# The first-token row and the first group's Newton steps on GpSimd instead of VectorE in an attention, Fourier-mix and FFN kernel

## The chip, the cores and the metric

The kernel runs on one core of a Trainium2 chip. The core has TensorE (PE, matmuls; PEld is its weight load), VectorE (DVE), ScalarE (ACT), GpSimd (POOL) and SyncE (SP, whose queue issues nearly all DMAs). Each engine works through its own instructions in the order in which they were put there; engines wait for each other by semaphores. The metric is the device time of one execution in microseconds (us); a shorter time is better.

## The reference

Input q, k, v of 4 batches, 8 heads, 768 tokens, head size 64; weights 512x2048 and 2048x512. All of it is float32.

```python
scores = scale * q @ k.T                       # per batch and head
keep = (pos_k < n_sink) | (0 <= pos_q - pos_k < window)     # 4 sink tokens, window 128
a = softmax(where(keep, scores, -1e9));  x = a @ v          # (4, 768, 512)
X = fft(fft(x, axis=1), axis=2);  u = x + real(X)
un = (u - mean(u)) / sqrt(var(u) + 1e-6)       # per token, over 512 features
out = u + relu(un @ w_ch1) @ w_ch2
```

## The kernel before

**Stages.** Each batch has six blocks of 128 tokens. The attention walks over 24 blocks x 4 pairs of heads = 96 steps, one step per pair of heads, about 2 us each, in the batch order of the program 0, 1, 2, 3. A step's chain is: PE scores (L703) into one of two PSUM buffers `s`; DVE merges the older keys (L709) and takes mask and row minimum (`soft1`, L721, twice per pair), which also frees the PSUM buffer; ACT takes the exponential (L727); PE transposes (L755, `pt`); ACT copies the result to SBUF (L762, `pta`); POOL cuts the window's edge out of it, once into a new tile (L771, `ptl`) and once in place (L779, `pta`); PE multiplies with v (L793, `xt`); DVE writes the block of x (`store_x`, L821) with the inverse sums (L743), which read what POOL prepared (L747, `mx`). POOL also makes the sink's two-part probabilities (L738, L739, `sk`).

**Fourier.** When four blocks of a batch are there, `fourier` books that batch's transform into later steps. Rows are folded (n against 768 - n, then m against 512 - m: L352, L359, L362, shared by DVE and POOL; in the last batch by DVE alone), split into two parts (L365 on ACT, L368 on DVE: `gh`, `gl`), multiplied with DFT constants on PE (stage 1, L395, results `za`, `zr`, `zb`, split again at L402 and L410; stage 2, L422 and L443), combined on DVE (L448, L449) and added to x (L459, L460, on POOL; in the last two batches also on DVE).

**The first token's row.** Token 0 takes no part in the fold; its attention row is worked out apart, goes through DRAM and comes back as `xr` in 33 partitions (`load_row`, L347). Then, once for each batch: `put_row` (L381) copies it into block 3 (`u[NHALF][0:1]`) once the first fold has read that block, `mid_sum` (L372) folds it, `mid_row` (L376, L378) splits it into `sph`, which the last matmul of stage 1 reads. They stand 5, 8 and 10 steps behind the start of the batch's folds (`ROW`), behind the step's other bookings for their engine.

**The first group's variance.** The FFN works on groups of blocks; the first has four (blocks 0 to 3 of batch 0). `normalize` books its statistics (steps 64 on), `deviations` (steps 72 to 80; the variance of 128 rows x 4 blocks becomes 1/sqrt by one integer guess, L522 and L524, and four Newton rounds of three operations, L527, L529, L531), `un_make` (from step 81 on, L539), the transposes and the two-part split (L545 to L554, `un_slots`).

**What sets the order.** Up to step 96 the order on each engine is written out (`SCHEDULE`: for each step, what comes in which order; a letter stands for the step's bookings for that engine). From step 97 (`CUT`) to the end of the first FFN group a scheduler sets the order; into that stretch fall the last batch's transform, the last attention blocks, the weights' conversion (`convert`, L591 to L593 on DVE, L608 on ACT, L609 on POOL) and the first FFN group (L620 and L1126 on PE). The rest of the FFN is again in written order.

Of the kernel before, what the change touches and what calls it, by code (L numbers as in the profile page):

```python
# [16 lines left out]
ALU = mybir.AluOpType  # L17
# [8 lines left out]
NHALF = NB // 2  # L26
# [8 lines left out]
NR = 33  # L35
# [28 lines left out]
F_N, F_M, F_S, ROW = (3, 3), (4, 5), (6, 7), (5, 8, 10)  # L64
# [142 lines left out]
def kernel(  # L207
# [17 lines left out]
    def f32(ap):  # L225
        return ap.bitcast(F32)
# [44 lines left out]
    def run(general):  # L271
        tag = "g" if general else ""
        with ExitStack() as p1:
# [8 lines left out]
            def at(s, eng, fn):  # L282
                ev.setdefault((s, eng), []).append(fn)
# [49 lines left out]
            def fourier(b, at, ready):  # L333
                u = uview(b)
# [32 lines left out]
                def fold_lo(j):  # L367
                    V.tensor_tensor(gl[:, j], t_.pop(("g", j)), f32(gh[:, j]), op=ALU.subtract)  # L368

                def mid_sum():  # L370
                    r = t_["x0"]
                    V.tensor_tensor(r[:, 1:256], r[:, 1:256], r[:, 511:256:-1], op=ALU.add)  # L372

                def mid_row():
                    t = t_["x0"]
                    V.tensor_copy(sph[:NR, :257], t[:, :257])  # L376
                    lo = sph[NR - 1:NR, :257]
                    V.tensor_tensor(lo, t[NR - 1:NR, :257], f32(lo), op=ALU.subtract)  # L378

                def put_row():  # L380
                    V.tensor_copy(u[NHALF][0:1], t_["x0"][0:1])  # L381

# [83 lines left out]
                for j in range(NHALF):  # L466
# [8 lines left out]
                    at(k + F_S[1], "V", lambda j=j: fold_lo(j))  # L475
                at(ready[0] + ROW[0], "V", put_row)
                at(ready[0] + ROW[1], "V", mid_sum)
                at(ready[0] + ROW[2], "V", mid_row)
                k = ready[2] + S1
# [37 lines left out]

            def deviations(b, blk, n):

# [5 lines left out]
                for _ in range(4):  # L525
                    yield
                    V.scalar_tensor_tensor(t, y, -0.5, x, op0=ALU.mult, op1=ALU.mult)  # L527
                    yield
                    V.tensor_tensor(t, t, y, op=ALU.mult)  # L529
                    yield  # L530
                    V.scalar_tensor_tensor(y, t, 1.5, y, op0=ALU.add, op1=ALU.mult)  # L531

# [26 lines left out]
            def normalize(s0, s1, s2, get_bank):  # L559
# [4 lines left out]
                for i in range(n):  # L564
                    at(s0 + 2 * i, "V", lambda i=i: stats(0, i, u[i], i, (0, 0)))
                steps = deviations(0, 0, n)
                for i in range(14):
                    at(s1 + i * (s2 - s1) // 14, "V", lambda: next(steps, None))
                for i in range(n):
# [769 lines left out]
```

## Time and profile before

| | us |
|---|---|
| time, median of 3 runs | 784.29 (782.91 to 787.69) |
| time of the profiled execution | 786.08 |
| its span, first to last instruction | 784.1 |
| PE busy | 755.7 (96%) |
| DVE busy | 453.5 (58%) |
| ACT busy | 237.1 (30%) |
| POOL busy | 185.1 (24%) |

The profiled execution lies 1.8 us above the median; 2.0 us of it lie around the span. Busy shares over the whole span say little here: the attention and the transforms fill the first 280 us, in which all engines work, and the FFN the rest, in which PE does nearly everything. So the stretches are read apart, by windows. PE's busy time takes the modelled ends of pipelined matmuls in, so that idle time of PE that does show is time in which nothing ran.

### The profile page before, as it was taken

What the parts mean: (1) busy time and instruction counts of PE and PEld (TensorE: products, weight loads), DVE (VectorE), ACT (ScalarE), POOL (GpSimd) and SP (SyncE); (2) the same over time, 40 slices, a digit from 0 to 9 for tenths busy, and PEclk for the clock granted to TensorE, in tenths of its full rate; (3) what the DMA queues carried; (4) which work ended last, traced back from release to release, by engine and by line L of the source; (5) the groups of instructions that cost most, each with busy time, mean ns of one, the idle gap of its engine ahead of it and who ended that gap; (6) DMA issues with size and microseconds to landing.
All of it is one profiled execution on the core that took longest, in us unless ns stands there. A gap on an engine that the chain in (4) does not pass through costs nothing.

```text
span 784.1 us, 11917 instructions
## 1 busy us (share of the span) xinstructions
PE 755.7 (96%) x4379; PEld 616.8 (79%) x4379; DVE 453.5 (58%) x1330; ACT 237.1 (30%) x704; POOL 185.1 (24%) x307
## 2 busy tenths in 40 slices
PE   7999998989998999999999999999999999999996
PEld 5676876867777878899888888888888888888895
DVE  6878587999999489561456424661456424611211
ACT  4887765766523123221111101111111111110110
POOL 2567477477654255100000000000000000000000
PEclk9999999999999899999999999999999999999998
DMA  9863535434215266110100002000200001000100
GB/s 283 268 177 105 151 83 177 127 112 145 86 50 166 92 196 208 66 59 1 54 0 1 1 18 89 1 0 1 81 0 1 2 1 54 1 0 1 54 1 31
DMA packets 41810, 57.67 MB, mean 74 GB/s; under 512 B 2796, under 2 KB 27500, under 8 KB 41360
## 3 DMA queue, kind: packets, MB, share of 16 engines
q1 hardware_dynamic: 41456, 53.07, 21.6%
q0 software_dynamic: 288, 3.76, 1.3%
q8 instruction: 36, 0.59, 0.3%
q14 instruction: 30, 0.25, 0.1%
HBM read 47.37 MB, written 9.45 MB: 72 GB/s over the span
## 4 chain that ended last, share of the span: by engine, by line
PE 80%; DVE 9%; POOL 4%; issue 3%; ACT 2%; DMA 2%; SPq 1%; POOLq 0%; DVEq 0%; ACTq 0%
PE o L1126 33%; PE h L620 33%; PE s L703 3%; PE xt L793 3%; PE pt L755 2%; PE za L395 1%; DVE cv L592 1%; DVE cv L593 1%; DVE sm L721 1%; PE zb L395 1%; ACT pta L762 1%; ACT sm L727 1%; DMA vt<-in_v_sink_dram 1%; POOL ptl L771 1%; DVE s L709 1%
## 5 line engine op out<-in xcount | busy, mean ns | idle before, releaser
L1126 PE MATMUL o<-w,h 128*128 128x512 f32 x876 | 218.6, 397 | 0.0
L1119 DVE SCALAR_TENSOR_TENSOR h<-h,h 128x512 fp32r<-128x512 f32 (+1 forms) x107 | 65.4, 611 | 250.5 <-ACT h L1114 250.3
L1126 PEld LDWEIGHTS o<-w,h 128*128 128x128 f32 x876 | 164.5, 190 | 36.0
L1114 ACT ACTIVATE h<-h 128x512 fp32r<-128x512 f32 (+1 forms) x107 | 57.1, 534 | 368.6 <-PE h L620 362.4
L620 PE MATMUL h<-un_slots,w 128*128 128x512 f32 (+1 forms) x576 | 124.7, 365 | 0.0
L620 PEld LDWEIGHTS h<-un_slots,w 128*128 128x128 f32 x576 | 99.6, 188 | 19.6
L620 PE MATMUL h<-un_last,w 128*128 128x512 f32 (+1 forms) x432 | 89.0, 355 | 0.0
L620 PEld LDWEIGHTS h<-un_last,w 128*128 128x128 f32 x432 | 72.7, 188 | 12.8
L727 ACT ACTIVATE sm<-sm,mx 128x132 f32<-128x132 f32 x192 | 76.0, 400 | 6.0 <-DVE mx L721 6.0
L1150 DVE STREAM_TRANSPOSE unf<-un 32x128 f32<-32x128 f32 x224 | 67.7, 302 | 3.2
L703 PE MATMUL s<-ring,q 64*128 64x260 f32 x320 | 49.9, 418 | 8.9 <-DVE mx L721 5.3
L721 DVE CUSTOM_DVE_ANT_0 sm<-s,mask 128x132 f32<-128x132 f32 x192 | 48.5, 293 | 6.3 <-PE s L701 1.3
L703 PEld LDWEIGHTS s<-ring,q 64*128 64x128 f32 x320 | 27.3, 188 | 21.6 <-issue 8.0
L609 POOL TENSOR_TENSOR w<-cv,w 128x512 fp32r<-128x512 f32 x25 | 34.1, 1366 | 30.5 <-ACT w L608 30.5
L793 PE MATMUL xt<-ptl,ldv 128*64 128x128 f32 x384 | 39.3, 285 | 0.2 <-POOL ptl L771 0.2
L727 ACT ACTIVATION_READ_ACCUMULATOR sm<-sm,mx 128x1 f32 x192 | 36.7, 191 | 0.0
L1126 PE MATMUL o<-w_ring,h 128*128 128x512 f32 x144 | 35.6, 393 | 0.0
L762 ACT COPY pta<-pt 128x512 f32<-128x512 f32 x48 | 28.0, 583 | 24.9 <-PE pt L755 23.5
L709 DVE COPY_PREDICATED s<-older,s 128x256 f32<-128x256 uint8 x80 | 33.7, 421 | 1.6 <-PE s L703 1.6
L771 POOL TENSOR_SCALAR_AFFINE_SELECT ptl<-pta 128x512 f32<-128x512 f32 x48 | 32.5, 678 | 7.3 <-ACT pta L762 7.2
L793 PEld LDWEIGHTS xt<-ptl,ldv 128*64 128x64 f32 x384 | 21.9, 136 | 15.1 <-issue 6.2
L793 PE MATMUL xt<-pta,ldv 128*64 128x128 f32 x320 | 31.7, 274 | 0.3 <-POOL pta L779 0.3
(197 smaller groups left out, 1039.4 us busy)
## 6 DMA issues: line engine op xcount, KB each, us to landing
raw<-in_moe_w_ch_dram SPq DMA_DIRECT2D x32, 512.0 KB, 3.7
ldv<-in_v_dram SPq DMA_DIRECT2D x28, 256.0 KB, 3.3
ring<-in_qk_dram SPq DMA_DIRECT2D x24, 264.0 KB, 4.8
out_dram<-u SPq DMA_DIRECT2D x24, 256.0 KB, 2.1
q<-in_qk_dram SPq DMA_DIRECT2D x20, 256.0 KB, 4.4
cst<-in_dft_dram POOLq DMA_DIRECT2D x1, 3348.0 KB, 12.8
ud<-us SPq DMA_DIRECT2D x12, 256.0 KB, 2.1
u<-ud SPq DMA_DIRECT2D x2, 1024.0 KB, 4.9
```

The lines of the kernel that those rows point to most:

```text
L620: T.matmul(ps[:, :tb], a[:, cs], x[:, :, cc, :], start=n == 0, stop=n == 3 * NCC - 1)
L703: T.matmul(ps[:, j, :P + W], st["q", g][rows, hp, :], keys(g, 2 * hp + j), start=True, stop=True)
L709: V.copy_predicated(ps[:, :, P + NS:P + W], older[qi > 2], ps[:, :, 0:P])
L721: V.tensor_tensor_reduce(sm[:, h % 4], ps[:, j, P:P + W], mask[min(qi, 3)], -SCALE, 3.0e38, ALU.add, ALU.min, accum_out=mx[:, 0, h:h + 1])
L727: A.activation(sm[:, h % 4], sm[:, h % 4], AF.Exp, bias=mx[:, 0, h:h + 1], scale=-1.0, accum_out=mx[:, 1, h:h + 1])
L762: A.copy(a, st.pop(("pt", g, hp // 2)))
L771: G.affine_select(lo, a, [[0, 4], [s, P]], compare_op=ALU.is_ge, fill=0.0, base=0, channel_multiplier=-s)
L793: T.matmul(ps[D * j:D * j + D, p, :], st["v", kb(g) - i][:, h, :], a[:, h % 4, :], start=i == 0, stop=i == n - 1)
L1114: A.activation(h[0], ps[:, :tb], AF.Relu)
L1119: V.scalar_tensor_tensor(h[1], ps[:, :tb], 0.0, f32(h[0]), op0=ALU.max, op1=ALU.subtract)
L1126: T.matmul(po[i], a[:, ts_], x, start=f == 0 and n == 0, stop=f == NF - 1 and n == 2)
L1150: V.transpose(unf[32 * q:32 * q + 32, :, r], un[r].rearrange("p (c q j) -> p c q j", c=NCC, q=4)[:, :, q])
```

## The change

`put_row`, `mid_sum` and `mid_row` are made by GpSimd, in the same steps, in all four batches. The twelve Newton operations of the first group are made by GpSimd too. The two fused operations of a round (scalar_tensor_tensor) are written with operations that GpSimd has: L527 becomes one tensor_tensor, L531 a tensor_scalar and a tensor_tensor, so a round has four instructions instead of three. The integer guess stays on VectorE, as do the deviations of the other groups and the general path.

```diff
+                R = V if general else G
+
                 def mid_sum():
                     r = t_["x0"]
-                    V.tensor_tensor(r[:, 1:256], r[:, 1:256], r[:, 511:256:-1], op=ALU.add)
+                    R.tensor_tensor(r[:, 1:256], r[:, 1:256], r[:, 511:256:-1], op=ALU.add)
 
                 def mid_row():
                     t = t_["x0"]
-                    V.tensor_copy(sph[:NR, :257], t[:, :257])
+                    R.tensor_copy(sph[:NR, :257], t[:, :257])
                     lo = sph[NR - 1:NR, :257]
-                    V.tensor_tensor(lo, t[NR - 1:NR, :257], f32(lo), op=ALU.subtract)
+                    R.tensor_tensor(lo, t[NR - 1:NR, :257], f32(lo), op=ALU.subtract)
 
                 def put_row():
-                    V.tensor_copy(u[NHALF][0:1], t_["x0"][0:1])
+                    R.tensor_copy(u[NHALF][0:1], t_["x0"][0:1])
...
-                at(ready[0] + ROW[0], "V", put_row)
-                at(ready[0] + ROW[1], "V", mid_sum)
-                at(ready[0] + ROW[2], "V", mid_row)
+                at(ready[0] + ROW[0], "V" if general else "G", put_row)
+                at(ready[0] + ROW[1], "V" if general else "G", mid_sum)
+                at(ready[0] + ROW[2], "V" if general else "G", mid_row)
...
-            def deviations(b, blk, n):
+            def deviations(b, blk, n, eng=V):
...
                     yield
-                    V.scalar_tensor_tensor(t, y, -0.5, x, op0=ALU.mult, op1=ALU.mult)
+                    if eng is V:
+                        V.scalar_tensor_tensor(t, y, -0.5, x, op0=ALU.mult, op1=ALU.mult)
+                    else:
+                        G.tensor_tensor(t, y, x, op=ALU.mult)
                     yield
-                    V.tensor_tensor(t, t, y, op=ALU.mult)
+                    eng.tensor_tensor(t, t, y, op=ALU.mult)
                     yield
-                    V.scalar_tensor_tensor(y, t, 1.5, y, op0=ALU.add, op1=ALU.mult)
+                    if eng is V:
+                        V.scalar_tensor_tensor(y, t, 1.5, y, op0=ALU.add, op1=ALU.mult)
+                    else:
+                        G.tensor_scalar(t, t, -0.5, 1.5, op0=ALU.mult, op1=ALU.add)
+                        G.tensor_tensor(y, t, y, op=ALU.mult)
...
-                steps = deviations(0, 0, n)
+                steps = deviations(0, 0, n, V if general else G)
                 for i in range(14):
-                    at(s1 + i * (s2 - s1) // 14, "V", lambda: next(steps, None))
+                    at(s1 + i * (s2 - s1) // 14, "V" if i < 2 or general else "G", lambda: next(steps, None))
```

Over the program DVE has 28 instructions less, POOL 32 more; the order on SP is the same, and on PE and ACT it differs only in the stretch that the scheduler orders. (The changed kernel's line numbers are 2 higher from `fourier` on, 9 higher behind `deviations`.)

The first place is POOL's order in the middle of the Newton rounds (`stat` is the tile of mean and variance), in the attention of batch 2. Before, three instructions stand between the last `sk` of a half block and the next:

```order
L738 CAST sk_2272<-sm_0_2167 128x2x16
L739 TENSOR_TENSOR sk_2272<-sm_0_2167,sk_2272 128x2x16
L771 AFFINE_SELECT ptl_3_2300<-pta_3_2266 128x512
L352 TENSOR_TENSOR f_2_0_2302<-u_65 128x512
L779 AFFINE_SELECT pta_3_2266<-pta_3_2266 128x512
L738 CAST sk_2272<-sm_2_2240 128x2x16
```

Of the change:

```order
L747 CAST sk_2271<-sm_0_2167 128x2x16
L748 TENSOR_TENSOR sk_2271<-sm_0_2167,sk_2271 128x2x16
L532 TENSOR_TENSOR stat_0_1899<-stat_0_1899 128x4
L534 TENSOR_TENSOR stat_0_1899<-stat_0_1899 128x4
L780 AFFINE_SELECT ptl_3_2300<-pta_3_2267 128x512
L539 TENSOR_SCALAR stat_0_1899<-stat_0_1899 128x4
L540 TENSOR_TENSOR stat_0_1899<-stat_0_1899 128x4
L352 TENSOR_TENSOR f_2_0_2304<-u_65 128x512
L788 AFFINE_SELECT pta_3_2267<-pta_3_2267 128x512
L532 TENSOR_TENSOR stat_0_1899<-stat_0_1899 128x4
L534 TENSOR_TENSOR stat_0_1899<-stat_0_1899 128x4
L747 CAST sk_2271<-sm_2_2239 128x2x16
```

So the rounds' instructions stand in pairs ahead of `ptl`, of the fold `f` and of `sk`; three of the eight pairs are in this piece.

The second place is POOL's order where `mid_row` of batch 1 falls, among the updates `u` of batch 0. Before:

```order
L459 TENSOR_TENSOR u_64<-u_64,d_1_1662 128x257
L460 TENSOR_TENSOR u_64<-u_64,d_1_1662 128x255
L771 AFFINE_SELECT ptl_3_1798<-pta_3_1765 128x512
L352 TENSOR_TENSOR f_1_2_1800<-us_2_1076,us_5_1079 128x512
L779 AFFINE_SELECT pta_3_1765<-pta_3_1765 128x512
```

Of the change:

```order
L461 TENSOR_TENSOR u_64<-u_64,d_1_1662 128x257
L462 TENSOR_TENSOR u_64<-u_64,d_1_1662 128x255
L378 CAST sph<-xr_1449 33x257
L380 TENSOR_TENSOR sph<-xr_1449,sph 1x257
L780 AFFINE_SELECT ptl_3_1798<-pta_3_1765 128x512
L352 TENSOR_TENSOR f_1_2_1800<-us_2_1076,us_5_1079 128x512
L788 AFFINE_SELECT pta_3_1765<-pta_3_1765 128x512
```

The two instructions of `mid_row` now stand ahead of `ptl`, a fold and `pta`; in batch 0 they stand ahead of the same three.

The third place is POOL's order where the scheduler has put the last batch's row. Before:

```order
L779 AFFINE_SELECT pta_3_3053<-pta_3_3053 128x512
L460 TENSOR_TENSOR u_65<-u_65,d_2_3141 128x255
L459 TENSOR_TENSOR u_65<-u_65,d_2_3141 128x257
```

Of the change:

```order
L788 AFFINE_SELECT pta_3_3057<-pta_3_3057 128x512
L383 COPY us_3_2624<-xr_3032 1x512
L374 TENSOR_TENSOR xr_3032<-xr_3032 33x255
L378 CAST sph<-xr_3032 33x257
L380 TENSOR_TENSOR sph<-xr_3032,sph 1x257
L462 TENSOR_TENSOR u_65<-u_65,d_2_3145 128x255
L461 TENSOR_TENSOR u_65<-u_65,d_2_3145 128x257
```

All four instructions stand together, behind the attention's last window cut and ahead of the updates.

## Rows read from the trace of the kernel before

**Rows 1.** Windows: us; per engine busy (xcount); granted PE clock, DMA share, GB/s.

```profile
100.00:140.00 40.00, 36.20 (x307) 27.61 (x307) 32.09 (x117) 24.99 (x95) 28.62 (x55) 1.00 0.49 148
140.00:164.00 24.00, 22.88 (x217) 18.55 (x214) 23.23 (x96) 16.77 (x63) 14.65 (x27) 1.00 0.32 92
164.00:181.00 17.00, 14.29 (x125) 10.70 (x123) 16.47 (x61) 11.44 (x43) 13.55 (x26) 1.00 0.40 128
200.00:254.00 54.00, 49.01 (x297) 41.31 (x295) 53.53 (x88) 19.91 (x45) 31.57 (x27) 1.00 0.33 106
254.00:261.00 7.00, 6.16 (x18) 5.24 (x19) 1.47 (x3) 1.73 (x4) 1.28 (x1) 0.51 0.27 92
280.00:784.00 504.00, 497.38 (x2353) 412.71 (x2351) 224.03 (x544) 77.37 (x141) 20.89 (x17) 1.00 0.10 34
```

**Rows 2.** PE's waits over the span: us in total, times, longest.

```profile
PE s L703 <- DVE mx L721: 5.3, 10, 2.6
PE a L422 <- DVE zb L410: 2.6, 1, 2.6
```

**Rows 3.** DVE's groups by form, 146.6 to 163 us: the first group's Newton operations.

```profile
L531 DVE SCALAR_TENSOR_TENSOR stat<-stat 128x4 f32<-128x4 f32 x4 | 2.5, 613 | 0.0
L529 DVE TENSOR_TENSOR stat<-stat 128x4 f32<-128x4 f32 x4 | 2.2, 546 | 0.1
L527 DVE SCALAR_TENSOR_TENSOR stat<-stat 128x4 f32<-128x4 f32 x4 | 1.1, 276 | 0.0
```

**Rows 4.** Timelines of POOL and of DVE (start, duration), around 153 us.

```profile
152.45 1.27 POOL L352 TENSOR_TENSOR f<-u 128x512 f32<-128x512 f32 x1
...
152.54 1.21 DVE L531 SCALAR_TENSOR_TENSOR stat<-stat 128x4 f32<-128x4 f32 x1
```

**Rows 5.** The row's operations by tile: ns min/median/max, first and last start.

```profile
L372 DVE TENSOR_TENSOR xr<-xr x4: 404/408/419, 60.2 to 212.8; 33x255 f32<-33x255 f32 x4
L376 DVE CAST sph<-xr x4: 281/296/722, 63.1 to 221.3; 33x257 fp32r<-33x257 f32 x4
L378 DVE TENSOR_TENSOR sph<-xr,sph x4: 417/418/737, 63.4 to 222.7; 1x257 fp32r<-1x257 f32 x4
L381 DVE COPY u<-xr x2: 404/406/408, 53.8 to 157.7; 1x512 f32<-1x512 f32 x2
L381 DVE COPY us<-xr x2: 405/406/408, 101.6 to 212.1; 1x512 f32<-1x512 f32 x2
```

**Rows 6.** POOL's groups by form: busy us, mean ns of one, idle before.

```profile
L771 POOL TENSOR_SCALAR_AFFINE_SELECT ptl<-pta 128x512 f32<-128x512 f32 x48 | 32.5, 678 | 7.3 <-ACT pta L762 7.2
...
L738 POOL CAST sk<-sm 128x32 fp32r<-128x32 f32 x48 | 11.5, 239 | 53.6 <-ACT sm L727 53.5
...
L359 POOL TENSOR_TENSOR f<-f 128x255 f32<-128x255 f32 x9 | 6.6, 738 | 0.8 <-DVE f L362 0.3
L747 POOL TENSOR_SCALAR mx<-mx 128x8 f32<-128x8 f32 x24 | 6.4, 265 | 2.0
```

**Rows 7.** Chain that ended last, 112 to 127 us: start, us, what.

```profile
112.29 0.22 POOL sk L738
...
126.11 0.60 POOL u L460
...
126.74 0.70 DVE bn L515
```

**Rows 8.** POOL's timeline in three places, idle time before in brackets.

```profile
64.01 0.66 POOL L738 CAST sk<-sm 128x32 fp32r<-128x32 f32 x1 [1.07 <-ACT sm L727]
...
67.12 0.82 POOL L779 TENSOR_SCALAR_AFFINE_SELECT pta<-pta 128x512 f32<-128x512 f32 x1
...
112.29 0.21 POOL L738 CAST sk<-sm 128x32 fp32r<-128x32 f32 x1 [2.14 <-ACT sm L727]
...
216.31 1.85 POOL L460 TENSOR_TENSOR u<-u,d 128x255 f32<-128x255 f32 x1 [4.43 <-DVE d L448]
```

**Rows 9.** PE's timeline: the matmul that reads that `pta`, and one at 254 us.

```profile
68.00 0.44 PE L793 MATMUL xt<-pta,ldv 128*64 128x128 f32 x4
...
254.84 1.66 PE L422 MATMUL a<-cst,za 128*128 128x258 f32 x6 [2.62 <-DVE zb L410]
```

**Rows 10.** DVE's timeline ahead of that matmul.

```profile
253.16 1.15 DVE L593 SCALAR_TENSOR_TENSOR cv<-raw,cv 128x512 int32<-128x512 int32 x1
254.23 0.55 DVE L410 TENSOR_TENSOR zb<-zb,zb 128x386 fp32r<-128x386 f32 x1
```

## The prediction

> **What bounds the kernel now.** I read the windows first, to see which stretch can move at all. From 280 us on PE works 497 of 504 us [rows 1]; none of the moved operations runs there, so that stretch only starts earlier or later. Before it, PE idles little: 3.8 us of 40 from 100 to 140, 1.1 of 24 to 164, 2.7 of 17 from 164 to 181, 5.0 of 54 from 200 to 254 [rows 1]. What DVE is relieved of can give back no more than such idle time, and only what DVE causes of it. PE's waits name DVE as the chief cause: 5.3 us in ten waits for the PSUM buffer that L721 frees, 2.6 us in one wait for L410 [rows 2]. DVE is full in 140 to 181 and 200 to 254 (39.7 of 41, and 53.5 of 54 us), POOL is not (28.2 of 41, 31.6 of 54) [rows 1]. That speaks for the change.
>
> Then I read DVE's and POOL's timelines side by side, because a busy DVE may be a waiting one. The Newton operation L531 at 152.54 has four numbers in each partition and takes 1.21 us; it ends at 153.75, POOL's fold, begun at 152.45, at 153.72 [rows 4]. The twelve operations take 5.8 us together (2.5, 2.2, 1.1), between 276 and 613 ns each on the mean of their line [rows 3], although they are all one size. So a DVE operation of this kind stands until the POOL instruction that began before it is through. That speaks against the change: what is put on POOL becomes something that DVE's other two-input operations (folds, splits, conversions) stand behind.
>
> The chain shows where POOL itself decides: from 112.29 to 126.71 it runs through POOL's instructions alone, until DVE's L515 at 126.74 [rows 7].
>
> **The change, part by part.** The sum is made against the profiled execution (786.1 us, 1.8 above the median of the runs).
>
> *Removed from DVE.* Four times `put_row` 0.41, `mid_sum` 0.41, `mid_row` 0.30 + 0.42 us: 1.53 us per batch, 6.1 in all at the medians [rows 5]; twelve Newton operations, 5.8 us [rows 3]. Together 11.9 us.
>
> *Added to POOL.* No row shows these forms there except one. `mid_sum` has the form of L359 but for fewer partitions: 0.74 us; the subtraction over 257 elements in one partition: the same 0.74. The copy of 512 elements lies between 0.27 (L747, 8 elements) and 0.68 (L771, 512): 0.68, by its length. The cast of 257 lies between 0.24 (L738) and 0.68: the middle, 0.46 [rows 6]. That is 2.6 us per batch (2.0 to 2.8), 10.5 in all. A Newton instruction on four elements lies between nothing and 0.68; the nearest row is L747 with 0.27 on eight, so sixteen take 4.3 us (0 to 10.9). Together 14.8 us.
>
> The Trainium skill's page "SBUF — State Buffer", section "Who interferes with whom", states that GpSimd and a VectorE instruction with two SBUF inputs exclude each other for whole instructions, and that whoever issues first blocks the other; the pair of rows at 152 us agrees (1.21 us for four elements). By that rule the move trades 11.9 us of DVE's time, part of it waiting, for 14.8 us in which POOL can block DVE; were this all, the sum would be +2.9 us instead of the one below.
>
> *Newton stretch and batch 2, 140 to 181.* POOL has 9.4 us free from 140 to 164 [rows 1], more than the 4.3 + 0.7 us it gets, and the result is wanted by L539 only in step 81. So nothing waits for it, and DVE loses 5.8 us of work ahead of the stretch in which PE idles 2.7 us [rows 1]. All of that is the most that can be won; nothing, if the folds behind the Newton operations stand behind POOL instead. I take two thirds, -1.8 us (0 to -2.7), since what is removed is twice the idle time. The row's own four operations of batch 2 I put at 0: POOL idles 3.4 us of the 17 from 164 to 181 [rows 1]; without that cover, +1.2.
>
> *Batch 1.* `put_row` and `mid_sum` come before POOL's 2.14 us of waiting that end at 112.29 [rows 8], and hide in them (1.42 us). `mid_row` stands in the run that the chain follows, ahead of `ptl`, a fold and `pta`: 0.46 + 0.74 = +1.2 us (0 if DVE's L515 has other cover, 2.6 if nothing hides).
>
> *Batch 0.* `mid_row` stands behind the `sk` at 64.01 and ahead of the `pta` cut that ends at 67.94; PE takes it at 68.00 [rows 8, 9], so there is no slack. +1.2 us, less what the cast at 64.01 gains when DVE's own two instructions are gone (0.66 against a mean of 0.24, [rows 6, 8]): +0.5 us (0 to 0.8). `put_row` and `mid_sum` fall ahead of POOL's 1.07 us of waiting.
>
> *Batch 3 and the conversion.* DVE is the bound there. It gives up 1.9 us (the cast took 0.72 here, [rows 5]). POOL takes its 2.6 us in 4.4 us of idle time ahead of 216.31 [rows 8], so no update is late; but DVE's folds, splits and conversions run at that very time and stand behind it. I take half of POOL's time as DVE's loss: -1.9 + 1.3 = -0.6 us (-1.9 to +0.7). It comes off the 2.62 us for which PE waits at 254.84 for L410 [rows 9, 10].
>
> *Sum.* -1.8 + 1.2 + 0.5 - 0.6 = -0.7 us: 785.4 us for an execution like the profiled one, **783.6 us** against the median. What is late next is the same as before: the scores' buffer in the attention, L410 at the end of the last transform.
>
> The page "GPSIMD Engine Reference" of the Trainium skill, section "Instruction dispatch", gives some 6 us, shown by no instruction of the profile, for the first call of a freshly loaded GpSimd kernel. A plain copy is new to POOL here; would it load one, the sum by that page would be up to +5.3 us. The trace of before cannot show it, since POOL makes no such copy there; it is no term of the sum.
>
> **Rivals.**
> 1. *The wait at 254.84 closes.* The clock granted to PE falls to 0.51, the lower of its two levels (1.2 instead of 2.4 GHz), from 254 to 261 us, just after PE had stood 2.62 us [rows 1, 9]. If DVE comes 2.6 us earlier, the 2.0 us that the forecast leaves of the wait go, and with them perhaps the low clock, worth 7 x 0.49 = 3.4 us: 783.6 - 2.0 - 3.4 = 778.2. For it: DVE is full all through. Against it: POOL's 2.6 us fall among DVE's two-input operations.
> 2. *The port is what counts.* The trade as the skill's rule has it, as a mechanism of this kernel: every new POOL instruction costs DVE its length where DVE is full. +2.9 us, 787.2. For it: the 1.21 us at 152.54 [rows 4]. Against it: before 140 us DVE isn't full (32.1 of 40, [rows 1]).
> 3. *Slower: POOL's queue decides.* Each `ptl` and `pta` behind a new instruction comes later, and PE with it. With nothing hidden that is 3 x 2.6 + 4.3 = 12.1 us, 796.4. It is slower by over 1% when 7.8 of the 12.1 us are not hidden. For it: the chain through POOL and the missing slack at 68.00 [rows 7 to 9]. Against it: POOL waits for ACT before it in most places (1.07 and 2.14 us, [rows 8]) and has 11.4, 9.4 and 3.4 us free in the three windows from 100 to 181 us [rows 1].
> 4. *Nothing is moved off any path*: the relief is hidden as the cost is, 784.3.
>
> **How the numbers follow.** Chances: the forecast, with rival 4 inside its own range of 781.5 to 786, 0.58; rival 1 0.14; rival 2 0.15; rival 3 0.10; anything else 0.03. 1% is 7.8 us, about what a measurement of this kernel can tell from no change: under 776.5 lies only a rival 1 that wins more than its 5.4 us (0.05); over 792.1 the greater part of rival 3 (0.07); within 1% 0.88. The range reaches from rival 1's 778.0 to 789.5, which is the sum with no relief at 140 to 181 and the upper bounds of the others (783.6 + 1.8 + 1.4 + 0.3 + 1.2 + 1.3 = 789.6); it leaves out rival 3's whole price and the far end of rival 1.
>
> **What would show it.** In the changed profile: the row's operations on POOL at about 0.7, 0.7, 0.5 and 0.7 us, the sixteen at about 0.3; DVE's busy time down by about 10 us; PE's idle time from 164 to 181 under 2.7 us; the run of POOL around 112 to 127 us longer by about 1; PE's wait for L410 around 254 us still there at 1 to 3 us, with the low clock behind it. The prediction is wrong if a POOL instruction on four elements takes over 0.5 us, if `pta` or `ptl` become PE's chief wait, or if the wait at 254 us and the low clock are gone.

## The result

The changed kernel is slower: **787.82 us** (median of 20 runs, 786.01 to 790.13) against 784.58 us (782.21 to 787.69) on the same chip, ratio 1.0043, 95% interval 1.0033 to 1.0053. That is 2.6 to 4.2 us lost where a gain of 0.7 was forecast. The time lies inside the range of 778.0 to 789.5 and within 1% of before, but it moved the other way than the forecast said. The profiled execution spans 785.7 us.

### The profile page after: what moved, and what is told of

Read it like the earlier page. It is cut to its first block, busy times and chain, and to the rows that moved or that the text cites. A ratio compares the mean times of both kernels' runs of the same rounds, so it can differ in the third digit from the quotient of the medians.

```text
span 785.7 us, 11920 instructions
## 1 busy us (share of the span) xinstructions
PE 757.0 (96%) x4379; PEld 619.1 (79%) x4379; DVE 448.6 (57%) x1302; ACT 236.8 (30%) x704; POOL 194.7 (25%) x339
## 4 chain that ended last, share of the span: by engine, by line
PE 81%; DVE 9%; ACT 3%; POOL 3%; issue 2%; DMA 1%; SPq 0%; DVEq 0%; ACTq 0%; POOLq 0%
PE o L1135 32%; PE h L629 32%; PE xt L802 4%; PE s L712 4%; PE pt L764 2%; PE za L397 2%; DVE cv L601 1%; DVE cv L602 1%; ACT pta L771 1%; PE zb L397 1%; ACT sm L736 1%; DVE cv L600 1%; DVE sm L730 1%; PE a L424 1%; DMA vt<-in_v_sink_dram 1%
## 5 line engine op out<-in xcount | busy, mean ns | idle before, releaser
L1135 PEld LDWEIGHTS o<-w,h 128*128 128x128 f32 x876 | 162.8, 188 | 35.5
L712 PE MATMUL s<-ring,q 64*128 64x260 f32 x320 | 49.3, 417 | 6.2 <-DVE mx L730 2.8
L730 DVE CUSTOM_DVE_ANT_0 sm<-s,mask 128x132 f32<-128x132 f32 x192 | 48.4, 292 | 8.0 <-PE s L710 3.1
L712 PEld LDWEIGHTS s<-ring,q 64*128 64x128 f32 x320 | 27.6, 188 | 17.9 <-issue 5.6
```

Source lines behind the costliest of these rows:

```text
L712: T.matmul(ps[:, j, :P + W], st["q", g][rows, hp, :], keys(g, 2 * hp + j), start=True, stop=True)
L730: V.tensor_tensor_reduce(sm[:, h % 4], ps[:, j, P:P + W], mask[min(qi, 3)], -SCALE, 3.0e38, ALU.add, ALU.min, accum_out=mx[:, 0, h:h + 1])
L1135: T.matmul(po[i], a[:, ts_], x, start=f == 0 and n == 0, stop=f == NF - 1 and n == 2)
```

## The profile after

In the changed kernel lines are 2 higher from `fourier` on and 9 higher behind `deviations`: L703, L721, L779 and L410 of before are L712, L730, L788 and L412 here, and the row's operations are L374, L378, L380 and L383. Kernels of the experiments with lines added are higher by a few more. From the page (busy us, share, instructions):

```profile
PE 757.0 (96%) x4379; PEld 619.1 (79%) x4379; DVE 448.6 (57%) x1302; ACT 236.8 (30%) x704; POOL 194.7 (25%) x339
```

The windows that answer to [rows 1], with the same columns:

```profile
100.00:140.00 40.00, 36.97 (x299) 28.64 (x297) 28.86 (x110) 24.06 (x89) 29.87 (x56) 0.91 0.43 131
140.00:164.00 24.00, 22.95 (x211) 18.76 (x209) 19.31 (x86) 17.39 (x67) 16.27 (x45) 1.00 0.42 119
164.00:181.00 17.00, 14.68 (x133) 11.25 (x130) 16.33 (x48) 10.06 (x39) 16.04 (x26) 1.00 0.35 114
200.00:254.00 54.00, 48.59 (x292) 41.86 (x293) 53.33 (x88) 19.82 (x47) 31.14 (x32) 0.97 0.28 88
254.00:261.00 7.00, 6.19 (x34) 5.22 (x33) 5.35 (x6) 3.10 (x7) 4.35 (x3) 1.00 0.67 225
```

The relief arrived: DVE works 19.3 us from 140 to 164 where it worked 23.2 [rows 1]. PE hardly used it: 22.95 us of 24 there, 22.88 before. The low clock at 254 to 261 is gone (1.00, 0.51 before), but there is one in the window from 100 to 140 (0.91) and one in that from 200 to 254 (0.97), where before there was none.

PE's waits over the span (us in total, times, longest), to be read against [rows 2]:

```profile
PE s L712 <- DVE mx L730: 2.8, 7, 0.7
PE xt L802 <- POOL pta L788: 2.7, 3, 1.4
PE za L397 <- ACT asb L433: 2.4, 1, 2.4
```

The wait for DVE halved (5.3 to 2.8 us), but most of that is not the change's. Half of the 5.3 us was one wait at 15 us, in the first block, before any operation that was moved:

```profile
15.02 2.13 PE L703 MATMUL s<-ring,q 64*128 64x260 f32 x8 [2.57 <-DVE mx L721]
```

The same place costs 0.56 us in the changed kernel and also in e11, which is the kernel before up to its Newton steps; so it differs between executions. From 46 us on the wait for DVE fell from 2.8 to 1.9 us. Waits for POOL's `pta` and for ACT's `asb` came instead.

Here is one such place in batch 0 and the same in batch 1: POOL's timeline, the matmul of PE that reads `pta`, and DVE's two waits that follow in batch 1 (start, duration, what; in brackets the idle time before it and what ended it).

```profile
65.12 0.39 POOL L378 CAST sph<-xr 33x257 fp32r<-33x257 f32 x1
...
68.39 0.63 POOL L788 TENSOR_SCALAR_AFFINE_SELECT pta<-pta 128x512 f32<-128x512 f32 x1
...
69.07 0.44 PE L802 MATMUL xt<-pta,ldv 128*64 128x128 f32 x4 [1.38 <-POOL pta L788]
...
118.12 0.86 POOL L378 CAST sph<-xr 33x257 fp32r<-33x257 f32 x1
...
121.93 0.63 POOL L788 TENSOR_SCALAR_AFFINE_SELECT pta<-pta 128x512 f32<-128x512 f32 x1
...
122.61 0.69 PE L802 MATMUL xt<-pta,ldv 128*64 128x128 f32 x4 [0.97 <-POOL pta L788]
...
125.98 0.20 DVE L752 RECIPROCAL mx<-mx 128x8 f32<-128x8 f32 x1 [2.64 <-POOL mx L756]
...
128.55 0.69 DVE L517 BATCH_NORM_STATS2 bn<-u 128x6 f32<-128x512 f32 x1 [2.37 <-POOL u L462]
```

In batch 0 PE took `pta` at 68.00 without a wait [rows 9]; now it stands 1.38 us. In batch 1 it stands 0.97 us for the same cut. DVE's wait for POOL's `mx` there was 0.70 us before and is 2.64 now; its wait for `u` is as long as before (2.38), and bn, which ended POOL's run at 126.74 [rows 7], starts at 128.55. About 0.7 us of that is the lag with which the changed kernel comes to 111 us (111.39 against 110.70 for PE's `x<-vs` matmul of the table below).

**Where PE stands.** To place each loss I took the start of PE's `x<-vs` matmuls, one for each block of the attention (the 24 rows of L807 in PE's timeline, L816 after). The table gives each kernel's lag against the kernel before at five of them, in us, set to zero at 46 us, ahead of the first place that mid_row touches; "low clock" is where the granted clock reads 0.5, the lower of its two levels (1.2 in place of 2.4 GHz), between 46 and 280 us. Each line is one execution.

```
kernel             at 74   at 111  at 138  at 194  at 215  low clock
before              0       0       0       0       0      254-261
after              +1.05   +0.95   +2.48   +2.60   +3.54   122-129, 232-235
e1 Newton only     +0.40   +0.45   +0.48   +0.15   +1.55   208-211, 259-262
e2 row only        +2.66   +3.67   +4.84   +4.26   +5.23   69-72, 233-236
e3 mid_row back    +0.37   +0.29   +0.29   +0.45   +1.74   204-207
e4 mid_row later   +0.21   +0.93   +3.54   +3.87   +4.82   133-136, 232-235
e5 mid_row early   +1.48   +1.42   +1.64   +1.75   +2.69   none
e6 mid_row b1      +0.37   +0.31   +1.48   +1.70   +3.09   206-209
e7 mid_row b0      +1.07   +1.00   +1.03   +1.21   +2.15   none
e8 mid_row b2,b3   +0.40   +0.29   +0.32   +0.49   +1.46   none
e9 placed          +0.53   +0.80   +0.98   +1.12   +2.07   229-233
e10 POOL more      +1.09   +1.08   +3.95   +3.96   +3.96   132-136, 259-262
e11 Newton one     +0.05   +0.30   +0.32   +0.07   +1.41   205-208, 256-260
e12 free only      +0.03   -0.09   +0.21   +0.38   +0.60   120-124
e13 batch 3 only   +0.04   -0.14   -0.18   -0.14   +0.81   none
e14 batch 3 back   +2.55   +4.09   +5.22   +5.29   +5.28   68-72, 260-263
```

The changed kernel loses 1.05 us in batch 0 (by 74), 1.5 in batch 1 (by 138), nothing that shows in batch 2, 0.95 in batch 3 (between 194 and 215).

Not all that moves a stand is the change. Kernels that are the same up to a place differ there by up to 0.4 us (e11 +0.30, e13 -0.14 at 111). Waits for DMA differ: before 111 us PE waits 1.2 us for one in the kernel before, 2.2 in e2 and 2.8 in e14; the 1.0 and 1.6 us more are what these two lose between 74 and 111. And a low clock moves the stand by itself: e1 and e11 have nothing moved in batch 3 and lose 1.4 us between 194 and 215, with a low clock there.

## The experiments

Each median is of 8 to 13 runs; the kernel before stood at 784.2 to 784.6 us beside them, and each ratio is to the kernel before on the same chip. In the expectations a theory is what was held to be so, a rival what speaks against it; their letters are explained where they first stand (C is one thing in e6 to e8 and another in e11).

**Which part loses: e1, e2, e3.** e1 moves only the Newton steps, e2 only the row's operations:

```
e1:  R = V                                      # the row's operations, steps booked on "V"
e2:  steps = deviations(0, 0, n)                # Newton steps on VectorE
```

> The first-token row's operations stay on VectorE; only the sixteen Newton instructions are on GpSimd. Theory M (PE waits for the window cut `pta`, because `mid_row` stands ahead of it on POOL in batches 0 and 1): 783.5 to 785.0 us, no different from before within 0.1%, since nothing of `mid_row` is on POOL. Rival N (the Newton instructions on POOL are what costs): 786.5 to 788. Rival P (every instruction moved to POOL costs VectorE its length, wherever it stands): about +1 us for 4.3 of the 14.8 us moved, 785.6.

> Only the row's operations (four per batch) are on GpSimd, the Newton steps are on VectorE as before. Theory M: the whole loss, 787 to 788.5 us. Rival N: 784 to 785.2. Rival P: 10.5 of the 14.8 us moved, so about +2.3 us, 786.9.

Measured: e1 784.07 us (ratio 0.9992, 0.9978 to 1.0006), e2 787.46 us (1.0037, 1.0025 to 1.0050). The loss is in the row's operations; the Newton steps show no loss, and a gain of up to 1.7 us is not excluded by e1's time alone (its stand, and e11, settle that). e3 puts only `mid_row` back:

```
- R.tensor_copy(sph[:NR, :257], t[:, :257])
+ V.tensor_copy(sph[:NR, :257], t[:, :257])
- R.tensor_tensor(lo, t[NR - 1:NR, :257], f32(lo), op=ALU.subtract)
+ V.tensor_tensor(lo, t[NR - 1:NR, :257], f32(lo), op=ALU.subtract)
- at(ready[0] + ROW[2], "V" if general else "G", mid_row)
+ at(ready[0] + ROW[2], "V", mid_row)
```

> The change with `mid_row` alone (cast and subtraction, four batches) back on VectorE; `put_row`, `mid_sum` and the Newton steps stay on GpSimd. Theory M: 784 to 785.3 us, PE no longer waits for `pta` at 67 and 122 us. Rival P: 4 x 1.4 + 4.3 = 9.9 of 14.8 us still moved, about +2.1 us, 786.7. Rival N: 786.5 to 788.

Measured: 784.34 us (1.0009, 0.9993 to 1.0025). Eight of the sixteen row operations and all Newton operations are on POOL here and cost nothing that shows (0.37 us by PE's stand at 74, see below), so theory P falls, whose 786.7 lies outside the interval. PE has no wait for `pta` left at 67 and 122 us. `mid_row` makes the loss.

**Is it the place: e4, e5.** The same line with mid_row's step at 12, behind `pta`, and at 8, directly behind `mid_sum`:

```
- F_N, F_M, F_S, ROW = (3, 3), (4, 5), (6, 7), (5, 8, 10)
+ F_N, F_M, F_S, ROW = (3, 3), (4, 5), (6, 7), (5, 8, 12)      # e4
+ F_N, F_M, F_S, ROW = (3, 3), (4, 5), (6, 7), (5, 8, 8)       # e5
```

> The change with `mid_row` still on GpSimd but booked two steps later (12 instead of 10), where it stands behind the cut `pta` and ahead of the next `sk`; all instructions and their lengths are the same. Theory M: batch 0's loss goes (POOL waits there for ACT), batch 1's mostly stays away from PE too: 784.5 to 786.3 us. Rivals N and P, for which the place doesn't matter: 787 to 788.5.

> The changed kernel with mid_row two steps earlier (ROW's last number 10 to 8): its copy and its subtract then stand on GpSimd directly behind mid_sum. In batch 1 that is just ahead of GpSimd's own pause (0.91 us at 112.1 in the changed kernel, 1.52 us in e4, each for ScalarE's sm), where nothing is queued behind them. Theory R (what costs is a longer unbroken run of GpSimd: in batch 1 it works without pause from 113 to 130, so 1.6 us more anywhere in it come out at the next ptl, pta and u): the pause takes them, 784.0 to 785.6, median of this kernel level with before, and no low-clock stretch between 118 and 137. Rival A (mid_row costs on GpSimd wherever it stands, through the copy's own length or what it does to other engines): 786.8 to 787.9 as in e2 and e4.

Measured: e4 787.73 us (1.0038, 1.0023 to 1.0052), e5 786.34 us (1.0031, 1.0016 to 1.0045). By the time, theory M falls in e4; in e5 the median lies between R's band and A's, and the interval reaches into both. PE's stand shows why: each cures one batch and not the other. e4 stands +0.21 at 74 (batch 0 cured) and loses 2.6 between 111 and 138, with a low clock at 133 to 136, which is a part of it; e5 loses only 0.2 between 111 and 138 (batch 1 cured), but has +1.48 at 74.

**One batch at a time: e6, e7, e8.** The changed kernel with mid_row on POOL in batch 1, in batch 0, in batches 2 and 3:

```
+ M = G if not general and b in (1,) else V       # (0,) in e7, (2, 3) in e8
- R.tensor_copy(...), R.tensor_tensor(...), "V" if general else "G"
+ M.tensor_copy(...), M.tensor_tensor(...), "G" if M is G else "V"
```

> The changed kernel with mid_row on GpSimd in batch 1 alone, in its place of the change; on VectorE in batches 0, 2 and 3. Theory R: batch 1 carries most of the loss, since GpSimd's run is longest there (folds of batch 1, updates of batch 0, attention): 785.8 to 787.3. Rival S (each batch pays its 1.2 to 1.6 us of GpSimd in part, evenly): a quarter of the 3.2 us, 785.2 to 785.6. Rival C (the loss is the place where the clock falls, and needs the delays of batch 0 and batch 1 together): 784.3 to 785.2 here and in e7.

> The changed kernel with mid_row on GpSimd in batch 0 alone. In the changed kernel's trace batch 0 loses about 1.2 us at 66 to 73 (PE waits for pta, which stands behind the copy and the subtract). Theory R: a part of that reaches the end, 784.3 to 785.8. Rival S: 785.2 to 785.6. Rival C: 784.3 to 785.2.

> The changed kernel with mid_row on GpSimd in batches 2 and 3 alone. In the changed kernel the lag against before stands at +2.2 us from 138 to 212 us, across batch 2's mid_row (172.7), although GpSimd has no pause there either, and grows to +3.3 at 215 (batch 3's). Theory R: the cost is only what PE then waits for, nothing in batch 2 and under 1 us in batch 3: 783.8 to 785.3. Rival S: two quarters of the 3.2 us, 785.9 to 786.5.

Measured: e6 785.73 us (1.0029, 1.0016 to 1.0043), e7 785.58 us (1.0026, 1.0009 to 1.0043), e8 784.63 us (1.0011, 0.9996 to 1.0025). Batches 0 and 1 carry it, 2 and 3 do not. C falls by e6's interval (785.4 us and more), while e7's still reaches into its band. S is not excluded by the times, but by the stands: in batch 2 (138 to 194) e8 loses 0.17 and e3 0.16, in batch 3 e8 loses 0.97 with mid_row on POOL and e7 0.94 without. (e8's expectation counts the lag from the start of the span, the table from 46 us.) By PE's stand against e3, whose mid_row is on DVE, batch 0's mid_row is worth 0.7 us (+1.07 against +0.37 at 74) and batch 1's 1.2 us (e6 loses 1.17 between 111 and 138, e3 nothing).

**Place chosen for each batch: e9.**

```
- at(ready[0] + ROW[2], "V" if general else "G", mid_row)
+ at(ready[0] + (12, 8, 10, 10)[b], "V" if general else "G", mid_row)
```

> The changed kernel with mid_row's step chosen batch by batch: 12 in batch 0 (behind the pta for which PE waited), 8 in batch 1 (behind mid_sum, in GpSimd's own pause), 10 as before in batches 2 and 3. All operations of the change stay on GpSimd. Theory R (each costs what the next ptl or pta comes later for PE, and nothing where GpSimd pauses before PE wants it): the stand of PE at 194 us is +0.4 to +1.0 over its stand at 46 us, against +2.6 in the changed kernel; median 784.4 to 785.6, from e3's level on. Rival A (mid_row costs on GpSimd wherever it stands): 786.5 to 787.9.

Measured: 785.31 us (1.0014, 0.9992 to 1.0036), PE's stand at 194 +1.12 in place of +2.60. Theory R's median holds, its stand is missed by 0.1; the interval alone reaches into A's band too. All operations of the change are still on POOL. e9 differs from e4 in mid_row's step in batches 1 to 3, and by the stands in batch 1 alone: 0.18 us lost between 111 and 138 against 2.61, and nearly the same in batches 2 and 3 (0.14 and 0.95 against 0.33 and 0.95). POOL's and PE's timeline of e9:

```profile
111.27 0.48 POOL L378 CAST sph<-xr 33x257 fp32r<-33x257 f32 x1
...
112.62 0.21 POOL L747 CAST sk<-sm 128x32 fp32r<-128x32 f32 x1
...
121.12 0.39 PE L802 MATMUL xt<-pta,ldv 128*64 128x128 f32 x4
...
126.21 0.64 POOL L462 TENSOR_TENSOR u<-u,d 128x255 f32<-128x255 f32 x1
```

and POOL's of e4:

```profile
113.05 0.21 POOL L747 CAST sk<-sm 128x32 fp32r<-128x32 f32 x1 [1.52 <-ACT sm L736]
...
122.52 0.39 POOL L378 CAST sph<-xr 33x257 fp32r<-33x257 f32 x1
...
127.89 0.63 POOL L462 TENSOR_TENSOR u<-u,d 128x255 f32<-128x255 f32 x1
```

In e9 mid_row fills the time in which POOL would have waited for ACT (in e4 the pause of 1.52 us is still there), `pta` at 121.12 is read without a wait, and the update on which DVE's bn waits starts 13.59 us behind the `sk` with which POOL's run begins (112.62 to 126.21), in e4 14.84 us (113.05 to 127.89). The medians differ by 2.4 us, the ratios to the kernel before by 1.9, with intervals that overlap. Of e4's 2.61 us by the stand the low clock at 133 to 136 is a part; e6, without one there, loses 1.17 us by mid_row at step 10.

**POOL's load by itself: e10.** Nothing is moved; POOL gets mid_row's two operations on top, in batches 0 and 1:

```
+ def more():
+     t, w = t_["x0"], fw.tile([NR, 257], F32R, tag="more", name=f"more_{b}", bufs=1)
+     G.tensor_copy(w, t[:, :257])
+     lo = w[NR - 1:NR]
+     G.tensor_tensor(lo, t[NR - 1:NR, :257], f32(lo), op=ALU.subtract)
...
+ if b < 2:
+     at(ready[0] + ROW[2], "G", more)
```

> The kernel before, with nothing moved, and in batches 0 and 1 a copy and a subtract of mid_row's shapes more on GpSimd, at mid_row's step, into a tile that nobody reads; VectorE keeps all of its work. Theory R (GpSimd's longer run alone makes the loss): the 1.2 to 1.6 us of batches 0 and 1 cost as in e6 and e7, 0.8 and 1.3 us by PE's stand, 785.7 to 787.0. Rival D (the loss comes of VectorE's order with the row's operations taken out, or of the row being ready later for PE): 783.6 to 784.8.

Measured: 786.92 us (1.0029, 1.0007 to 1.0051): theory R by the time. By the stand batch 0 pays 1.09 us where 0.8 was expected and batch 1 2.87 where it was 1.3; 0.77 of the 2.87 are there by 127 us, ahead of the low clock at 132 to 136. DVE keeps its program, and the waits of the changed kernel are there again (PE's and DVE's timelines of e10):

```profile
68.99 0.44 PE L801 MATMUL xt<-pta,ldv 128*64 128x128 f32 x4 [1.09 <-POOL pta L787]
...
122.86 0.44 PE L801 MATMUL xt<-pta,ldv 128*64 128x128 f32 x4 [0.98 <-POOL pta L787]
...
126.24 0.20 DVE L751 RECIPROCAL mx<-mx 128x8 f32<-128x8 f32 x1 [2.55 <-POOL mx L755]
...
130.70 0.44 PE L401 MATMUL za<-cst,gl 128*128 128x386 f32 x1 [1.21 <-DVE gl L368]
```

The path is: `pta` late, the scores' chain late, POOL's `mx` (1.85 us more wait than before) and its updates late, DVE's bn (at 128.83, behind POOL's `u`) and `gl` directly behind it late, and PE stands 1.21 us for `gl`, where it stood 0.6 before.

**Is DVE's relief worth anything: e11.**

```
- for _ in range(4):
+ for _ in range(1 if (b, blk) == (0, 0) else 4):
```

> The kernel before with one Newton round in the place of four for the first group (three rounds, nine operations of VectorE at 147 to 163 us, are left out, so its deviations are rougher); GpSimd has nothing more to do. Theory C (VectorE is not what PE waits for there, so that its relief turns into its own pauses): PE's stand at 184 us within 0.3 us of the kernel before's, 783.6 to 784.8. Rival B (the relief is worth the 1.8 us of the prediction, and in e1 GpSimd's sixteen operations took it back): PE stands 1.2 to 1.8 us earlier at 184, 782.0 to 783.0.

Measured: 785.01 us (1.0000, 0.9976 to 1.0025); PE's stand at 184 and at 194 is +0.07. The median lies 0.2 us above theory C's band, and the interval reaches to -1.9 us, so the time alone doesn't tell C from B; the stand is C's, and B's 1.2 to 1.8 us are not there. A window of e11:

```profile
140.00:164.00 24.00, 22.88 (x215) 18.31 (x214) 20.26 (x88) 16.50 (x62) 14.80 (x28) 1.00 0.32 95
```

DVE's longest wait there, from 140 to 184 us (us in total, times, longest):

```profile
DVE d L448 <- PE b L443: 2.4, 1, 2.4
```

DVE has 3 us less to do (20.26 against 23.23, [rows 1]), PE does exactly as much in that window as before (22.88), and DVE now waits 2.4 us for PE. POOL has nothing more to do here, so it ate no gain; there was none of that size. From 138 to 184 PE gains 0.25 us (+0.32 to +0.07) and in e1 0.33, less than what executions of one program differ by.

**Batch 3: e13, e14.** The row's operations on POOL in batch 3 alone, Newton steps on VectorE (e13); the changed kernel with batch 3's row back on VectorE (e14):

```
- R = V if general else G
+ R = G if not general and b == 3 else V          # e14: b < 3
```

> The kernel before with the row's operations on GpSimd in batch 3 alone, and nothing else moved (Newton steps on VectorE). Theory T (in batch 3 VectorE's folds and conversions run beside GpSimd's new work and take twice as long, so the transform starts later; what VectorE was relieved of shortens the wait behind L410 afterwards): PE's stand at 215 us +0.9 to +1.0 later against its stand at 46, PE's wait at 254 us 0.8 to 1.7 in place of 2.6, median 784.0 to 785.3. The prediction's term for batch 3 (-0.6): no later at 215, 783.0 to 783.9.

> The changed kernel with the row's operations of batch 3 back on VectorE; batches 0 to 2 and the Newton steps stay as changed. Theory T: PE's stand at 194 us as in the changed kernel (+2.3 to +2.8), nothing more of it at 215, the wait of 2.6 us at 254 back: 786.5 to 787.9, within 1 us of the changed kernel. The prediction's term for batch 3 taken away would leave 788.4; if batch 3 made the loss, 784.2 to 785.2.

Measured: e13 784.41 us (1.0006, 0.9992 to 1.0020), e14 787.30 us (1.0036, 1.0024 to 1.0048): theory T's times both times. In e13 PE's stand at 215 is +0.81, in place of +0.9 to +1.0, and +0.95 over its stand at 194. In e14 nothing more is lost at 215, as expected, but the stand at 194 is +5.29 in place of +2.3 to +2.8: it has a low clock at 68 to 72, which the changed kernel has not, and waits 2.8 us for a DMA before 111 us. Batch 3 is worth about nothing, the sum of a loss and a gain. The loss, on DVE's timeline before and after:

```profile
212.42 0.40 DVE L359 TENSOR_TENSOR f<-f 128x255 f32<-128x255 f32 x1
212.75 0.40 DVE L372 TENSOR_TENSOR xr<-xr 33x255 f32<-33x255 f32 x1
213.08 0.41 DVE L591 TENSOR_SCALAR cv<-raw 128x512 int32<-128x512 int32 x1
213.42 0.67 DVE L821 TENSOR_TENSOR us<-x,mx 128x512 f32<-128x512 f32 x1
```

```profile
214.42 0.83 DVE L600 TENSOR_SCALAR cv<-raw 128x512 int32<-128x512 int32 x1
215.17 0.94 DVE L359 TENSOR_TENSOR f<-f 128x255 f32<-128x255 f32 x1
216.03 0.88 DVE L601 SCALAR_TENSOR_TENSOR cv<-raw,cv 128x512 int32<-128x512 int32 x1
216.83 0.68 DVE L830 TENSOR_TENSOR us<-x,mx 128x512 f32<-128x512 f32 x1
```

POOL runs 214.17 to 217.49 without pause there:

```profile
214.17 0.79 POOL L383 COPY us<-xr 1x512 f32<-1x512 f32 x1
215.05 0.78 POOL L374 TENSOR_TENSOR xr<-xr 33x255 f32<-33x255 f32 x1
215.89 0.47 POOL L378 CAST sph<-xr 33x257 fp32r<-33x257 f32 x1
216.44 1.05 POOL L380 TENSOR_TENSOR sph<-xr,sph 1x257 fp32r<-1x257 f32 x1
```

DVE's conversion takes 0.83 where it took 0.41, its fold 0.94 where it took 0.40, and where the row's two operations stood there is now a second conversion operation (L601), ahead of the block's `us`, on which the transform waits. e13, with nothing else moved, has the same order and lengths. The gain comes later: PE waits less for L412; that it comes of conversions done earlier is not shown by itself. PE's waits of e13 from 215 to 275 us:

```profile
PE za L397 <- ACT asb L433: 2.4, 1, 2.4
PE a L424 <- DVE zb L412: 1.7, 1, 1.7
```

The wait behind L412 is 1.7 where it was 2.62 [rows 9], 0.8 in the changed kernel; a wait of 2.4 for ACT, which the kernel before has not, has come instead. In e14 the 2.6 us are back.

**What is free, together: e12.** Newton steps on POOL, the row's operations on POOL in batches 1 and 2, mid_row of batch 1 at step 8:

```
- R = V if general else G
+ R = G if not general and b in (1, 2) else V
- at(ready[0] + ROW[2], "V" if general else "G", mid_row)
+ at(ready[0] + (10, 8, 10, 10)[b], "G" if R is G else "V", mid_row)
```

> Only what cost nothing by PE's stand: Newton steps on GpSimd, the row's operations on GpSimd in batches 1 and 2 alone, with mid_row of batch 1 at step 8; batches 0 and 3 keep theirs on VectorE. Theory R: level with the kernel before, 783.6 to 785.0; no gain either, since VectorE's relief is not waited for. Rival A: a part of the loss for each batch moved, 785.2 to 786.2.

Measured: 785.58 us (1.0019, 0.9994 to 1.0044). Inconclusive: the median is 0.6 us above theory R's band and inside A's, the interval takes in both, the stand (+0.38 at 194) agrees with R. No version faster than the kernel before was found.

## Why the prediction was wrong

*Newton stretch, -1.8 us forecast, nothing clear of noise measured.* This is the step that failed: DVE's relief was counted as PE's time. "All of that is the most that can be won ... I take two thirds": PE's 2.7 us of idle time from 164 to 181 were put down to DVE, because DVE was full. PE's waits there do name DVE. From 164 to 181, before:

```profile
PE s L703 <- DVE mx L721: 0.8, 2, 0.7
PE a L422 <- DVE d L449: 0.8, 1, 0.8
PE unx L545 <- DVE u L821: 0.5, 1, 0.5
PE s L703 <- DVE mx L743: 0.5, 1, 0.5
```

and in e11, with nine Newton operations less on DVE:

```profile
PE unx L545 <- DVE u L821: 0.9, 1, 0.9
PE a L422 <- DVE d L449: 0.8, 1, 0.8
PE s L703 <- DVE mx L721: 0.2, 1, 0.2
```

The waits for the scores' buffer shrink by 1.1 us, the one for `u` grows by 0.4, the one for `d` stays, and DVE itself waits 2.4 us for PE. PE gains 0.25 us in e11, 0.33 in e1 and nothing in the changed kernel (+2.48 at 138, +2.60 at 194). So a wait that names DVE was not one that less work on DVE closes. The 5.3 us that the prediction put ahead of this reading were for half the one wait at 15 us, which no moved operation could reach.

*Batch 1, +1.2 forecast, +1.2 measured* for mid_row alone (e6), 1.5 in the changed kernel, which also has the low clock of 122 to 129 there. The step is right, also in its mechanism and in that `put_row` and `mid_sum` hide: e3 loses nothing between 74 and 138, and POOL's pause of 2.14 us [rows 8] is 0.91 in the changed kernel.

*Batch 0, +0.5 (0 to 0.8) forecast, +1.05 measured.* Mis-sized. Its own terms give 1.2 less 0.42 (0.66 - 0.24), which is +0.8 and not +0.5. That there is no slack at 68.00 was read rightly, and mid_row alone is 0.7 us, by e7 against e3; e10, which keeps DVE's own two instructions and so gets nothing back on the cast, pays 1.09. What was missed is `mid_sum` and `put_row`, costed at nothing. e3, e6 and e8, with these two alone on POOL in batch 0, stand at +0.37 to +0.40 at 74; e11, e12 and e13, with nothing moved there, at +0.03 to +0.05. (e1, with nothing moved there either, stands at +0.40 for another reason: PE waits 0.47 us for a DMA at 52 us.) The pause that follows them did not take them up, as these rows of the changed kernel's POOL show:

```profile
59.79 0.91 POOL L374 TENSOR_TENSOR xr<-xr 33x255 f32<-33x255 f32 x1
...
64.44 0.39 POOL L747 CAST sk<-sm 128x32 fp32r<-128x32 f32 x1 [1.07 <-ACT sm L736]
```

It is 1.07 us long as before [rows 8], but ends at 64.44 in place of 64.01: ACT's result, which ends it, is late as well (what delays it these rows do not show).

*Batch 3, -0.6 forecast, about 0 measured* (e13 +0.24 us; its interval, 0.9992 to 1.0020, just reaches -0.6). The contention was seen and sized at 1.3 us; what was not seen is that the order of DVE's conversions moves, with 0.95 us lost at 215, and that ACT's `asb` is late next.

The corrected sum, 0 + 1.5 + 1.05 + 0, is +2.55 us, at the lower end of the measured 2.6 to 4.2; what is left over is open, and the last section says where a part may lie. Since the two gains were 2.4 us of the sum and neither shows, the sign turned. (Two ends of the range were carried over unlike their sums, 778.0 for 778.2 and 789.5 for 789.6, and the measurement told 0.4% from no change, where the prediction thought 1% its limit; neither matters here.)

*The rivals.* Rival 3 is the mechanism that happened, `pta` as PE's wait and POOL's queue behind it, at a quarter of its full price, since POOL's pauses hide the rest, as the prediction said against it. Rival 2's time (787.2) is near the measured one by luck, and its reason is not what happened: e1 puts sixteen new POOL instructions where DVE is full and is level, e3 has 24 of the 32 there and is level, and the same eight instructions of mid_row cost or don't by their place. DVE's operations do take twice as long beside POOL's in batch 3 (0.94 us for 0.40). The Trainium skill's page "SBUF — State Buffer", section "Who interferes with whom", states that GpSimd and a VectorE instruction with two SBUF inputs exclude each other for whole instructions; the fold's rows at 215 us agree, but by e1 and e3 the +2.9 us by that rule were not the cause of the loss. Rival 1's wait closed (2.62 to 0.8) and its low clock went, which the prediction had named as a sign of being wrong, but neither paid: another wait and two other low stretches came.

*What was to show it.* The prices on POOL were right. Those of the row's operations by tile (ns min/median/max; `us` left out, two more copies), and the slowest of the four lines of the Newton operations by form (count, busy us, mean ns):

```profile
L374 POOL TENSOR_TENSOR xr<-xr x4: 714/751/906, 59.8 to 215.0; 33x255 f32<-33x255 f32 x4
L378 POOL CAST sph<-xr x4: 392/432/856, 65.1 to 215.9; 33x257 fp32r<-33x257 f32 x4
L380 POOL TENSOR_TENSOR sph<-xr,sph x4: 724/729/1052, 65.6 to 216.4; 1x257 fp32r<-1x257 f32 x4
L383 POOL COPY u<-xr x2: 599/599/599, 55.3 to 161.3; 1x512 f32<-1x512 f32 x2
```

```profile
L534 POOL TENSOR_TENSOR stat<-stat 128x4 f32<-128x4 f32 x4 | 1.4, 340 | 0.3
```

0.75, 0.73, 0.43 and 0.60 us against 0.74, 0.74, 0.46 and 0.68; the Newton operations 0.20 (three of the lines) and 0.34 against 0.27. The first copy of GpSimd (55.29 us) takes 0.60 like the next and starts directly behind the fold that ends at 55.34, so no cost of a first call appeared. (The Trainium skill's page "GPSIMD Engine Reference", section "Instruction dispatch", gives some 6 us for the first call of a freshly loaded kernel; the trace shows none here.) DVE's busy time fell by 4.9 us (453.5 to 448.6) where 10 were expected: what stayed on DVE takes some 5 us longer in sum, the folds 2.5 of it, which agrees with their standing beside POOL. PE's idle time from 164 to 181 is 2.3 us, under 2.7 as said, though none of it came out as a gain. POOL's run in batch 1 is 1.1 us longer (112.99 to 128.55 against 112.29 to 126.74), where 1 was expected. `pta` is PE's second wait (2.7 us), close behind the scores' buffer (2.8), and that was a sign of being wrong too.

## What to carry to other kernels

An engine that is 97% busy is not yet the one that is waited for: before work is moved off it, take some of that work out (as e11 does) and see whether the engine that sets the end moves. The name behind a wait doesn't settle it either. For the engine that takes the work, what counted here was not its busy share but whether it pauses between the new instruction and the next thing that another engine wants from it. The same two operations of 1.2 us cost 0.2 us by PE's stand inside POOL's pause (e9, batch 1) and 1.2 in its run (e6). And a pause covers work only where what ends it does not come late too, as it did in batch 0.

## Not expected of the hardware

Where the low clock falls differs from execution to execution. Before, its one stretch between 46 and 280 us was at 254 to 261; it begins at 254.2, inside PE's wait of 2.62 us. e12 has that wait as well (2.62 us) and a full clock there. In e2 and e14 a low stretch begins at 68.9 and 68.4, where PE's wait of 1.4 us for `pta` ends (68.73 and 68.53); the changed kernel, with the same program and wait, and e7 have none there. In e4 and e10 one begins at 133.0 and 132.3, some 2 us behind the wait of 1.2 us for `gl`; e6 has that wait and no low clock behind it. So one delay of about 1 us costs 1 us in one execution and 2.7 in another (+1.05 in the changed kernel, +2.66 in e2 at 74), which no sum over durations foretells; why the low clock comes here and not there stays open.

It also goes with most of the spread between runs. Runs of the kernel before by mean granted clock: 0.998 and over, median 782.6 us (30 runs); 0.993 to 0.997, 784.5 (78); 0.992 and under, 787.6 (12). Of the changed kernel: 786.1 (3), 787.7 (10), 788.5 (7). The first two groups differ by 3.5 and 3.2 us between the kernels, so the loss is not the clock's alone; the last differ by 0.9, of few runs. But the changed kernel has 7 of 20 runs in the lowest group and the kernel before, beside the experiments, 12 of 120, so a part of the 3.2 us may come by the clock. That is not shown.
